# Which engine turns the attention outputs of four units: TensorE or the transposing DMA

## The chip, the cores and the metric

The kernel runs on one core of a Trainium2 chip. The metric is device time in microseconds (us). The core has five engines with queues of their own: TensorE (PE; its weight loads are shown apart as PEld), VectorE (DVE), ScalarE (ACT), GpSimd (POOL) and SyncE (SP), which here only issues DMAs. Sixteen DMA engines move the data.

## The reference

The inputs are q, k and v with 8 batches, 8 heads, 576 positions and 64 features per head, and two weight matrices, 512 x 2048 and 2048 x 512. Attention is computed twice: on averages of four neighbouring positions, and locally with a band of three positions to each side. Both results are added, and a dense part follows.

```python
def sm_attn(qq, kk, vv):
    s = scale * np.matmul(qq, kk.transpose(0, 1, 3, 2))
    s = s - np.max(s, axis=-1, keepdims=True)
    a = np.exp(s)
    a = a / (np.sum(a, axis=-1, keepdims=True) + 1e-09)
    return np.matmul(a, vv)
...
out_up = np.repeat(out_d, factor, axis=2)          # out_d = sm_attn of the averages, factor 4
...
scores = np.where(mask, scores, -1000000000.0)     # mask: |i - j| < 4
...
return (out_up + out_local).astype(np.float32)
...
h = x @ w_in                                       # x: 4608 tokens x 512
g = h - np.tanh(h)
return (g @ w_out).astype(np.float32)
```

## The kernel before

The work is cut into 32 *units*, each one batch and two heads: units 4b to 4b+3 are batch b. A unit goes through these steps (`attention`, L490 to L802):

- q and k are loaded by SP (L358, tiles st; some in Tw), cast to bf16 (L516, qr) and turned so that features lie on partitions: in units 0 to 7 by TensorE (L523), from unit 8 on by a transposing DMA (L567, kq; L561 for the remainder rows rr of a batch, which are loaded at L370 into sr and cast at L506).
- the averages' q and k are formed (L604, L609 and others), TensorE forms the scores (L667, L677, L683; these matmuls use 64 rows), ACT the exponentials (L688, L692, L696, tile E), DVE or GpSimd multiplies by the band mask (L723).
- TensorE multiplies by v (L737; v is loaded at L382, cast at L442, and averaged by L473 on TensorE or L454 and L458 elsewhere). DVE takes the reciprocal of the sums (L753) and normalises into `ln`, six blocks of 128 x 128 with tokens on partitions (L755).
- ln has to be turned so that features lie on partitions, and the local result and the average's result are added into `xT`, in two instructions (`join`, L773).

The last step has two forms, chosen per unit by the table `BACK`. With 1, TensorE turns the six blocks into PSUM (L780), ACT or DVE copies the averages' part to SBUF (`od`, L784 or L786), and DVE joins from PSUM. With 0, SP issues one transposing DMA from ln to `lT` (L792), and DVE or GpSimd joins from SBUF:

```python
lambda: nc.sync.dma_start_transpose(
    out=lT[s].rearrange("p (n c) -> p n c", c=128),
    in_=ln[s].rearrange("p n c -> p (n c)"))
```

The tiles ln, lT, od and E have two buffers each, used by even and odd units.

The dense part of batch b (`mm1`, L814) multiplies the 512 main tokens of the batch, from xT, by w_in in 16 groups of four matmuls with 512 columns; ACT takes tanh (L826), DVE subtracts (L829, tile gT). It needs xT of all four units of its batch. The remaining 64 tokens of two batches go together (L841, L852, L854). The second product runs for the batch before in the meantime: plain (L895) for batch 0, from batch 1 on with seven products of half size (L1035; the sums of quarters that it needs are made by L944 and L970, the results put together by L1056, L1059 and L1106); L867 is that of the remaining tokens. Stores are issued at L925 and L883.

No loop sets the order. Every step is recorded as an operation with what it reads and writes, and four tables of text then say everything else: `TURNS` is the order in which all 2,199 operations are emitted, for all engines and SP's queue; `ENGINES` picks an engine for each operation that has a choice; `BANKS` picks the PSUM bank; `FILL` places idle matmuls (L1244, on a tile of zeros), and `BEHIND` adds waits between certain operations. Each engine works its own instructions in this order, and SP issues its DMAs in it, so that an instruction that waits holds what stands behind it on the same engine.

Of the kernel before, what the change touches and what calls it, by code (L numbers as in the profile page):

```python
# [101 lines left out]
def kernel(  # L102
# [44 lines left out]
    REL = [  # L147
# [4 lines left out]
    ]  # L152

    TURNS = (
        "0003070G0H0I0J060E0F0K0L04050Q0R0O0P0W0X010e0f0C0M0N0S0T100Y0Z110g0h020a0b1215130D0A160U"
        "0V171H1P18141I0B1J190m0n1L1Q1A1K1R221M1N0i0j1O242R231T1j1k1B251S1C1f1g1u1U0c0d1W1v1w2S1y"
        "0k0l1x2Z091V2I2J0y2T082G2H1z1D2V291E2W0o0p261F1d1e2U1X1l1m212X27201n1o2z1Y2b1Z0z391p1q2a"
        "0q0r2d282c2n2o1r1G2e311h1i1s2f2p2q2g2A2K2L322Y1t3A3B2B2O2y5H2C3C3D302D2P3G5I332E1a353E0s"
        "0t2M2N5J34362v2h2F373N3O5K5L5P2i1b5e5f380u0v3F5M5S2w5N2r2s2j5O5Q3H5U5R3I3J5v662Q2k683K5B"
        "5T1c635E5V3L3d2l5C5x2m643j3k5y3M3l3e5D5F3f3g5X3p3q5W0w0x3m3h3v3r3n3w3i3P3Q5w3s5Y3t2t2u3o"  # L160
        "413x615k5l3y3u5z3z4243604744404D4E4548623T3U495Z654A464F4G4B4J6b5a4K4H4L4M3V3W674N4C6e4P"
        "6c6B4Q5g5h4I4R4S2x694V3R3S4O4W6g4b5b6T4X4c5c6A4T4Y5d4h5s4Z4U6V4i6U4j5t5m5n4k4a4d4e4l4n6W"
        "3X3Y4o4f4p4q4m6C6d4r6X6D4t6Z4u6E6Y4v7A4w4z6a505G4g51526F7B536f6G554s4x3Z3a56576Q6j6H3b3c"
        "587f7C6h7g6R54597D7E4y887F6i8d7G895A7I7H8e6k5u966l976m6y9C736z6n717J7475728E7K7l7L7m7677"
# [12 lines left out]
        "9R9SDPDVErEsDQDLJxDWDpDRDXJRDbG7G8FuEGDcDYG5G6DkDdDqFXFYDlGJIQDeDmGOIiIjJSEZGTDnDrDsGUFd"
        "GHMvMwFLGZFvGIINGcIOGhGiGaHhFmHmGbGuFMEtGnFNF6GzGsH0FwFOFPGAFxH5IuIqHrHAIRFyFzIvHCJ1ITHD"
        "ISJ2HIGBGCGtHNIxIyIVHwHSJ3IUHUJkJlJ4FQHVIkIlHaJ5JGJHG0IWJ7JEJFJ6HfIIJTJUGDIXIrGEHgHBGKGF"
        "IYJoJpGLIzJ8IoIpGMJXGGGPKLKMJ0GQGNK0K1GVJyJ9GWJAGRGdJYIsItGeGXGSHTJZGfGYGjJbGkJaGgJMGoHx"  # L180
        "JzGvJVGpGlK6K2K3GwGqI0K7I5JdGmMYIZIaIAGxGrMZIBJWH1MWGyJqJrH2ICH6JOJPH3JNH7JBJCJsK8H8JcHE"
        "KAHFImInJtK9K4HJJuJvH4NAHKKCJmJnJeH9IbMaMbHGHOJfHPHLHHMeHWK5KJKKHMHXHbJKJLJgMfHcHQHiHYKB"
        "HRJhJiHjMgHdHZHnHkMrMsHeHsMhMzN0HtHlHoMtMuHuKuKDHpI1I2HvKRM4I3NBM5HqMcMAJDNCNDMiI6KEI7I4"
        "KZNGKTKUI8KaKFJIJJJQKbKcDgDhNHMdI9KwKGKHKxKSL2KvMkL3IDIEMXKhMjKiKjL9KkMlLAKpLPMmJwNhKsKt"
        "LQMnKqKrLVNgLWNZNaJjNILbMBN5NiNjNEN6LdNKKILeNJLjNbNTNULkNMNLN7N8KVMxMyLpKWNmNNKPKQL8QmLr"
        "N1N2KXNnLsOCNdNeNFLBNOQnMoMpNPLCLqLHNkLIKYNlOFOGLxOLNoLNKdLOKNKONsLyRDREKlNqM3KmOMNQNRNp"
        "KeMGODKyKnONOEKfKoMJLcOHOIOPKzKgOOL4MKNrNVNWL0L5N3N4OQLDL6MPO1O2L1N9NcLENzO0MqMQL7LFRLRM"
        "NtORLGLJO7LKNuNvLRO8LLLSNSOJLXLMNwNxLTLYMROSOKQwLULfLlOTLZLgOUV1LtQxLhLuLaOVOWLmRTLiQyLv"
# [12 lines left out]
        "WfWiWWWsWxWoWlWOWpWyWqWPWjWrWtWgX4WhXAXqWbX5WwX6XFX1X3X7X8WzXNWuX0XSX9WvXEXXXJXOXBXKXLXC"
        "XMXPXGXfXQXTXDXgXkXhXRXUXWXYXVXbXrXHXlXcXsXIXvX2XiY0XZXdXmXaXeY5XtXjXuXwY1XnYAY6XxYFYbXy"
        "YGXzY9YEY2YHXoY3YIYBYJYCYOY4YPYcYdYDYKYQYLYRYSXpYMYNYTYUYVYeYWYfYgYXYYZ2YZYaYjYkY7Y8Z3Yi"
        "YlYwYxYyYhYzYmZ0Z4Z5YnZ7YoYpZ1YqZ6YrZAZ8Z9YsYvZBYtYuZCZDZJZEZKZHZFZGZOZIZPZQZRZSZLZMZN"
    )
    ENGINES = (
        "APADDADAADPPDDPPDDADDDDAPPDADDAADDDPDDDDDAADDAPAADDDAAADDDPPAPPPAADAPPPDDDAAPADADPPPPDAA"
        "PADAAAPPPDDAPDPDAAPPDPDAAAADPPAADDAADDDDDPDPDDPPDAAAPPAAPPDDAAPPPAAPPDDPPADDDDDPPPAPPAAP"
        "PDPPPAPPAAPDDPDDAPDAADPDDPDAPDPAADPDDDPDDDDDPPPAPPAAPPDPPPADDAADDDPPPAPPAAPPDDDDAPPPDADD"
        "PDPPADDDDDDDPAPPAAPPDPDDAPPAAPPDPDPAPPAADDDDPPPDPPAADPDPPPDDDDDDPPAPPAAPPDPPPAPPAAPPDPPP"  # L210
        "APPAAPPDDPDADPDAAPPDDDPADDDDDPPPADPAAPPDPDDAPPAADPDPPPDPAADDDPPPPPDDDDPPPAPPDDD"
    )
    BANKS = (
        "0123453012067016731120212706021330112130022310312010301210031220313200320131002302101322"
        "1203320110023110230110023110012310201302020100121030123101321321310021010113021310213211"
        "0301213001210301230110210123110321132010310213021031032011003210310121021010120031010210"
        "1010300123001230012301230123746524173025604276540257613"
    )
    FILL = (
        "15717 2b71 2A71 3B41 2D11 5S31 3H31 6671"  # L220
    )
    BEHIND = (
        "0211 1H12 1D1V 0z20 1t2f 5I30 5Q5N 635B 5w5W 6562 7H6i 7271 9UCH ABAA AmAF DtAL BiCJ F7C"
        "Z FgEm IHFJ IPG9 JxFt EtGb IrJ6 MYK7 NAK4 KRKu NhLA QnOC OMLO NcOQ OXNy V2Oo RYR1 RZP7 O"
        "BP8 SVSU SdSW V6V5 R8TR RkVZ VmVz VlWE"
    )

    const = ctx.enter_context(tc.tile_pool(name="const", bufs=1))
# [257 lines left out]
    def attention(p):  # L486
# [276 lines left out]
        def join(eng, loc, pool):  # L763

            for t0, step, nt, n, o in ((1, 28, 3, 28, 144), (0, 114, 2, 30, 512)):
# [7 lines left out]
                eng.tensor_tensor(out=dst, in0=src, in1=add, op=ALU.add)  # L773
        if BACK[p]:
            bname = ("bk", p)
# [500 lines left out]
```

## Time and profile before

| what | value |
|---|---|
| median of 3 runs | 311.13 us (311.07 to 311.53) |
| the profiled execution | 311.1 us, its span 309.4 us |
| granted TensorE clock | 1.0 |
| busy PE, DVE, ACT, POOL | 299.1, 248.2, 213.5, 165.0 us |
| transposes L780 on TensorE | 72 matmuls, 219 ns each (units 0 to 11) |
| transposing DMAs lT<-ln, L792 | 20 (units 12 to 31) |
| first L814 starts, last TensorE instruction starts | 30.16 us, 305.44 us |

The table's busy times come from the profile page, the clock from the list of cores, and the starts from the timeline. A matmul's time counts until its result is out, while the next one starts earlier: matmuls with 512 columns are shown with 379 ns each, and follow each other at a distance of 216 ns. A step's share of TensorE's time is therefore read from the distance of starts.

### The profile page before, as it was taken

The page shows a single profiled execution, that of the slowest core. Times are in us where ns is not written, and L with a number is a line of the kernel's source. Part 1 is how long each engine was busy: PE and PEld are TensorE (multiplying, and loading weights), DVE is VectorE, ACT ScalarE, POOL GpSimd, SP SyncE. Part 2 cuts the span into 40 slices and gives each one's busy share as a digit, 9 for nine tenths or more (in the row PEclk, how much of TensorE's full clock was granted, in tenths as well). Part 3 has the DMA queues.
Part 4 walks back from the last instruction along what each step waited for, and adds up shares of the span by engine and source line. Part 5 has one row for each costly group of instructions (what it writes and reads, how often), then busy time and mean ns, then how long its engine had stood idle before and what let it go on. Part 6 is the DMA issues. An engine that isn't in the chain of part 4 may idle for free.

```text
span 309.4 us, 7786 instructions
## 1 busy us (share of the span) xinstructions
PE 299.1 (97%) x2969; PEld 198.6 (64%) x2980; DVE 248.2 (80%) x450; ACT 213.5 (69%) x380; POOL 165.0 (53%) x213
## 2 busy tenths in 40 slices
PE   8878999999999999999999999999999999999995
PEld 3656555455677666875587665657868655567784
DVE  2687887689998889999897888989897987745644
ACT  2778776288888777988966977887768875445210
POOL 5437795026764476338761477485553580517900
PEclk9999999999999999999999999999999999999999
DMA  7999999999999999999999989999998733000134
GB/s 223 249 246 237 242 243 166 206 219 258 253 244 286 228 216 301 219 230 221 201 219 277 224 192 207 261 270 270 173 251 152 174 95 95 0 0 3 51 122 136
DMA packets 120870, 60.81 MB, mean 197 GB/s; under 512 B 88832, under 2 KB 118528, under 8 KB 120832
## 3 DMA queue, kind: packets, MB, share of 16 engines
q1 hardware_dynamic: 115968, 55.53, 78.3%
q0 software_dynamic: 4224, 4.19, 8.5%
q10 hardware_dynamic: 640, 0.59, 0.6%
q8 instruction: 23, 0.38, 0.5%
q14 instruction: 15, 0.12, 0.1%
HBM read 44.04 MB, written 9.44 MB: 173 GB/s over the span
## 4 chain that ended last, share of the span: by engine, by line
PE 90%; DMA 3%; SPq 3%; DVE 1%; issue 1%; ACT 0%; DVEq 0%; ACTq 0%
PE ps L814 36%; PE ps L1035 28%; PE ps L737 5%; PE ps L841 5%; PE ps L867 4%; PE ps L895 4%; PE ps L667 3%; SPq L382 2%; DMA st<-in_k_dram 2%; DMA sr<-in_k_dram 1%; PE ps L780 1%; PE ps L683 1%; SPq L358 1%; PE ps L473 1%; PE ps L677 1%
## 5 line engine op out<-in xcount | busy, mean ns | idle before, releaser
L814 PE MATMUL ps<-xT,w_in_sb 128*128 128x512 bf16 x512 | 122.4, 379 | 0.0
L829 DVE TENSOR_TENSOR gT<-ps,u 128x512 bf16<-128x512 f32 x128 | 84.6, 685 | 19.0 <-ACT u L826 18.3
L826 ACT ACTIVATE u<-ps 128x512 f32<-128x512 f32 x128 | 74.5, 601 | 33.4 <-PE ps L814 29.7
L814 PEld LDWEIGHTS <-w_in_sb 128*128 128x128 bf16 x512 | 47.9, 98 | 46.9
L1035 PEld LDWEIGHTS <-gT 128*128 128x128 bf16 x672 | 64.4, 98 | 15.8
L1035 PE MATMUL ps<-w_out_sb,gT 128*128 128x256 bf16 x336 | 43.4, 273 | 0.0
L1035 PE MATMUL ps<-Tw,gT 128*128 128x256 bf16 x336 | 42.8, 273 | 0.0
L516 POOL CAST qr<-st 128x512 bf16<-128x512 f32 x40 | 24.1, 615 | 20.6 <-DVE gT L970 6.2
L688 ACT ACTIVATE E<-ps 128x912 bf16<-128x912 f32 x32 | 29.7, 930 | 3.0 <-PE ps L677 2.2
L755 DVE TENSOR_TENSOR ln<-ps,r 128x768 bf16<-128x768 f32 x32 | 30.6, 956 | 1.0 <-DVE r L753 0.2
L594 ACT COPY kt<-kq 128x576 bf16<-128x576 bf16 x23 | 27.2, 1188 | 0.7 <-DMA kq<-qr 0.5
L737 PEld LDWEIGHTS <-E 128*128 128x128 bf16 x576 | 21.4, 97 | 5.3 <-DVE E L723 0.8
L723 DVE TENSOR_TENSOR E<-E,mask 128x1152 bf16<-128x1152 bf16 x29 | 23.5, 813 | 1.4 <-ACT E L688 0.7
L773 POOL TENSOR_TENSOR xT<-lT 128x336 bf16<-128x336 bf16 (+1 forms) x24 | 15.9, 684 | 14.8 <-DMA st<-in_k_dram 4.7
L604 POOL TENSOR_TENSOR half<-kq 128x576 f32<-128x576 bf16 x15 | 19.2, 1281 | 5.9 <-DVE v L454 1.8
L696 ACT ACTIVATE E<-ps 128x576 bf16<-128x576 f32 x32 | 20.8, 651 | 0.3 <-PE ps L683 0.3
L609 POOL TENSOR_TENSOR qkd<-half 128x288 bf16<-128x288 f32 x21 | 16.8, 799 | 6.9 <-DVE gT L970 4.2
L1106 POOL TENSOR_TENSOR y<-y,keep 128x512 f32<-128x512 f32 x12 | 15.3, 1273 | 9.5 <-ACT y L1056 9.5
L737 PE MATMUL ps<-vw,E 128*128 128x65 bf16 x320 | 18.9, 193 | 1.2 <-DVE E L723 0.8
L1056 ACT COPY y<-ps 128x512 f32<-128x512 f32 x19 | 11.1, 585 | 11.0 <-PE ps L1035 10.7
L854 DVE TENSOR_TENSOR gL<-ps,u 128x512 bf16<-128x512 f32 x16 | 15.8, 1013 | 2.3 <-ACT u L852 2.3
L737 PE MATMUL ps<-vpr,E 128*128 128x65 bf16 x128 | 16.3, 194 | 0.0
(127 smaller groups left out, 469.6 us busy)
## 6 DMA issues: line engine op xcount, KB each, us to landing
vst<-in_v_dram SPq DMA_DIRECT2D x56, 160.0 KB, 4.1
st<-in_q_dram SPq DMA_DIRECT2D x28, 256.0 KB, 4.4
st<-in_k_dram SPq DMA_DIRECT2D x28, 256.0 KB, 5.0
out_dram<-y SPq DMA_DIRECT2D x14, 512.0 KB, 3.6
v<-in_v_dram SPq DMA_DIRECT2D x20, 256.0 KB, 4.0
w_in_sb<-in_moe_w_in_dram POOLq DMA_DIRECT2D x4, 512.0 KB, 9.4
w_out_sb<-in_moe_w_out_dram POOLq DMA_DIRECT2D x4, 512.0 KB, 8.0
vr<-in_v_dram SPq DMA_DIRECT2D x8, 128.0 KB
```

The costliest lines, as they stand in the source:

```text
L516: (eng, ns, lambda dst=dst, src=src, fn=fn: fn(out=dst, in_=src), port)
L594: ("ACT", 1180, lambda: A.copy(out=ktv, in_=src), False),
L604: eng.tensor_tensor(out=half, in0=flat[:, 0:576], in1=flat[:, 576:1152], op=ALU.add)
L688: A.activation(out=E[s][:, :, E0:E0 + 456], in_=at(s1)[:, :, PS0:512], func=AF.Exp, scale=SCALE)
L696: A.activation(out=E[s][:, :, EP:EW].rearrange("p h (i c) -> p h i c", i=2)[:, :, :, 0:G], in_=at(s2)[:, :, 120:408].rearrange("p h (i c) ...
L723: eng.tensor_tensor(out=el, in0=el, in1=mask.unsqueeze(1).to_broadcast([128, 2, S]), op=ALU.mult)
L737: T.matmul(po[:, hh, 65 * n:65 * n + 65], E[s][:, hh, e:e + 128], vv, start=start, stop=stop)
L755: op("DVE", 960, lambda: V.tensor_tensor(out=ln[s].rearrange("p n (h d) -> p h n d", d=D), in0=blocks()[:, :, :, 0:64], in1=r[s].unsqueeze ...
L814: T.matmul(at(name)[:, 0, :], w_in_sb[:, dc, fc * 128:(fc + 1) * 128], xT[dc][:, c0:c0 + S].rearrange("p (c g) -> p c g", c=4)[:, :, 0:128 ...
L826: op("ACT", 600, lambda: A.activation(out=u[us], in_=at(name)[:, 0, :], func=AF.Tanh), reads=[("hd", kb, fc)], writes=[("u", us)], uses=[n ...
L829: op("DVE", 690, lambda: V.tensor_tensor(out=gT[g][:, fc, :], in0=at(name)[:, 0, :], in1=u[us], op=ALU.subtract), reads=[("hd", kb, fc), ( ...
L1035: T.matmul(dst, left[:, f, 128 * j:128 * j + 128], right[:, f, :], start=(first and e == 0 and f == 0 and (j == 0 or apart)), stop=(e == 1 ...
```

## The change

The entries of `BACK` for units 8 to 11 (batch 2) become 0: their six transposes each on TensorE, the copies od and the joins from PSUM are left out, and four transposing DMAs L792 with joins from SBUF take their place.

```diff
-    BACK = [c == "1" for c in "11111111111100000000000000000000"]
+    BACK = [c == "1" for c in "11111111000000000000000000000000"]
...
     TURNS = (
-        "0003070G0H0I0J060E0F0K0L04050Q0R0O0P0W0X010e0f0C0M0N0S0T100Y0Z110g0h020a0b1215130D0A160U"
...
+        "00040O0P0B0I0J0Q0R0K0L0G0H010E0F0g0h030W0X0C0e0f050M0N02100Y0Z1H151I0m0n1J1L0c0d1K221M0o"
...
     FILL = (
-        "15717 2b71 2A71 3B41 2D11 5S31 3H31 6671"
+        "15714 1351 1771 2T41 1E71 1X51 2b71 2h71 5S41"
```

The other tables are new as a whole: TURNS, ENGINES, BANKS and BEHIND differ from the first entry on, so every engine's order differs, in the opening as well as in the units that the change of BACK doesn't touch. The number of operations is the same in kind apart from the step described; TensorE has 2,954 matmuls in place of 2,980 (24 transposes and 2 fillers fewer), SP issues 250 DMAs in place of 246. Line numbers of the changed kernel are one lower behind the tables.

What stands differently around the places of the change: of the four new joins two are on DVE and two on GpSimd; L784 (od on ACT) occurs 5 times in place of 1, and L786 (od on DVE) 3 times in place of 11; masks on DVE 30 in place of 29. SP's first loads are those of unit 1 and then unit 0, in place of 0 and then 1, and GpSimd issues three of the four loads of w_in one after the other, where casts stood between them.

More of the change, by code (lines that the diff above doesn't have):

```diff
@@ L160 @@
[L160 to L164, printed above, removed]
@@ new lines @@
+        "0p1116231O13121N1714240k0l181P19091A0A0U0V2S1R1Q250S0T1T2R0D0a0b082T1u262V2U1S1j1k1W071f"
+        "1g06391B1C2W1U2G2H1v1w270i0j1D1y1x2Z1l1m1z1d1e0y2X201V2I2J1E291n1o1F282z1X1h1i2a211p1q3A"
+        "2Y2b0z3P3Q2c1Y2d1Z0q0r1r2n2o315e5f2e0s0t1s2g1G2A3N3O0u0v2f3B2y2p2q3C303D332t2u5H2B3E2O2C"
+        "341a3G322D2M2N351t2P3F2h1b372v365P5J1c2w382i5I5S5Q2j3H2E2Q5K2F2k5U5R5E3I3J5L5B2l5T5N5C5F"
+        "3K2K2L5X5D2m3d3e3L5V3f3M3j0w0x3p5M3k3q5W3r5O3g3l3m3h5v5Y3n3i643v3w3x3o3y633s413z5Z42655a"
@@ new lines @@
+        "433t445x47485y406T495b456U3u662r2s4A614D5c6b4J4B5d4K4E46684F4G4L5w5g5h4C674H4M3V3W5k5l4P"
+        "4V4N4W3T3U3X3Y4Q6B4R4O3R3S4S6V4T6X4I5m5n4X4Y694b5i5j4U2x4h6W4i5z6Y4j4Z4c604k4n6A624d4e4l"
+        "6e6Z4o4a5G6g4p5s4m4t6c4u6a4v4f5t4q6d4z504r4g6C7B6f6D4w7A6E51554x523Z3a566j574y6F3b3c5853"
+        "4s6Q7f6h7C7g596G6i886H6R7D547E897F5A8d8e5u72967I6k737G8E716l76776y7l6z7m7H7475976m8j9T7J"
+        "9U9V6K6L9C7K9D7L5q5r8k6I6J6n6s6t7M6o8p5o5p7N6p7r7O6O6P8q787s6M6N9f798F8K9g6u6v8vCB8w9a6q"
@@ new lines @@
+        "6r8L8xCC9h9v9w9i7X9jCF6w6x7YCG9t9u7x9k7Z8Q9Z8R6S7a9b9c9I8S9l7y9W9mCE7b7R7S9X7hCD7V7W7z9n"
+        "7P7Q70AB7c9o7i9x9y9pAA7d9JBD7jACAD7n7e7o9YCH9O9d9P9q9rCI7p7t7kA7AG9eAdA3A4A87u9QB4B5807v"
+        "AH817qB0B1Ae84829zA0Ah85AgA1A2AI83868A7T7U9s7wAJ8BAiAj878GAK8HAEAL8MAVAW8I8NAFATAUAM8V8J"
+        "B2B3AoAm8CANBGBHAq8D8ZAn8WAO8OAP8aBFAp8X8f8PDtAQAR8b8gBE8YAk8l8h8mBM8cBIBJ8rAr8i8s8n8yAs"
+        "8T8UAt8zAbAc8t928oDxBcBdAu908uDyEHEI93AlBN919899AvDuAw9E94AS9F9A9K95AxAyBKBOEb9GBP9L9BEa"
@@ new lines @@
+        "A9DzE0BqE3Br9M9HBsBQB8B9BtE49NCLBaBbBRBAAXAYBTByBSBzELEMBLCJC0A5A6C1EPEQCMBBCKC6E5E6CRE7"
+        "C9CACSC7C8CYE1BUEcEdCZE2CoBVCpAzBWCuE8CvEABXBYE9D0EiDvAfD2EJEKD3BiEkD8BeBfBjEgD9AZAaEBEh"
+        "DEBkBlEVEjENEODGIFElF7EuEvDHCXEmDMB6B7EnDNF8EeCaBZF9FAEfCbECCgFDEDBmEwExBCBuDSG3G4BvEWBn"
+        "IgIhFEBwC2FeBoC3IGFhFiBxFfFFC4FGChBpF2FICNERESFHC5FgCTCnCUFjFkFKCOCmCcFJCdFTFUCVEoF3EXEY"
+        "CPCWCiD19R9SCeCjCQIcIdCqCrDFCfF4F5CkCwBgBhCsEpCxClIeIfD4IHFBCtCyD5EEEFDAEqFnD6DBDTDCCzDU"
@@ new lines @@
+        "IJFlDZD7IKFCDaDDDIFoDODfDwFpIwFqDVFrFZILIMDJIPDPFsFaDKDiETEUFtDjFuEyEzDWMUDQDLDoIQF0F1Dp"
+        "DXDRFXFYG9DbFRFSDqDcEGDkG5G6DdDYDlErEsFLDeDmJSGJFMF6JxGODnFbFcGTEZG1G2GHGUG7G8FvGZIiIjGI"
+        "HhINDrDsGcIOGhGaGiGnGbGuGsFNIvGzFmH0EtFwH5FOFPFxHmHAHrGtFdIRFyFzHwITHCJ1IVFVFWHDISGAHIIx"
+        "IyJ2HNJRJ3IqHSIUJTJUJ5HUJ7FQHVJ4HaJkJlG0HfIkIlIWIuJ6IsItGDIIHgGKKLKMIrGLJyIzJGJHIXIYGEGM"
+        "HTGBGCGPGFJEJFGQGNJ8IZIaJXGRGGGVJ0GWJ9JAGdJYGeGXGSMVJZGfJzGYGjJaMWK2K3GkGgGoGlHxHBGpK0K1"
@@ new lines @@
+        "JVGvGmGqI0JMGwJWMzN0JNI5K6IADgDhJbIBIoIpGrK7GxH1H2JdMYGyH6H3JsICH7K8MZH8HEJcMaMbK9HJK4HF"
+        "H4MeKCJeJoJpH9HGHKJOJPHOMfJfHLImInHHHPKAHWJmJnIbHMHQHXJKJLHbK5HRJBJCHiKBJgHjHYHcIDIEHnHZ"
+        "HdJuJvHoHkHeMgMtMuNAHsHpHlKJKKJtHtMkMrMsKuI1MiI6JIJJHuI2HqNBJQKDJDNCNDI7McHvM4I3M5I8KRI4"
+        "KNKOMAMdKZJhJiKSKaI9NGKbMhKcKTKUKEKFKhNHJwKiKjMjKGKHKkKvKwKpKxKPKQNEL2KqKrL9NFL3JqJrMlLA"
+        "MxMyLPMmNgLQKsKtMnLVNhNTNULWJjMBLbNIN5LdN6NiNjNJKILeLjNKOCLkNMMvMwNLKVNZNaLpKWNmNNRDREL8"
@@ new lines @@
+        "OELrN7N8KXNOLsNPMoMpNnMXLxLyLqNkKYLBN3N4M3NoNbLCMGNqLHNsNcNdNeLIOLNlOFOGKdKlOMKeLOLNNVNW"
+        "KmNpKyNQNRODKzKnNrMJONO1O2L0KoLcMKOHOIOOL1MPMQKfO7NtN1N2MRN9QmL4OcOdKgO8L5ORNzO0QnLDNuMq"
+        "L6NvO9OALJLKOPLEL7LLNwNxLROQLFLXLSLGNSRHRILYLTOSLMOJLfOTOKQwLgLULlOULmLZQxLtLhLaOVOWLuRT"
+        "QyLnLiOgLzLvLoM0QrOiOjR0M6LwM1HyHzQqM7MCM2NyQsQtM8MDMLM9MEMMRSR2OqMFOhRURVOvMNOXP0QzP1MO"
+        "RFRGOkP6OoOlRBRCOrNfOaObOwOpOmOsNXNYOxOYOZOtP9OnRlRmQoQuPEOySHSIPFOuPKQvRNR9RAOzP2O5O6RO"
@@ new lines @@
+        "PAPPP7PBRnRoPGRPRQPCR1P3MSMTPHPDRYP4O3O4PLPIR3P5RWPSRZR4RXPMR5S4PYPTPJR6R7PNPZS5RaPUPOPd"
+        "PaRyPVPeRcRzPlPbPfPqOBS0S1RbPmPgPvP8PwPnMHMIQ3RdReRpRqQ4PxPoPrOeOfRtS6SqSrPsPySUPRQ5PtPW"
+        "RuSXSYS7Q8PQPXPcQpSJSKQFV6SNSOPhRfSVS2Q9SdS3PjPkQ6SeQGQAPpV1SARgV2PuRhSWQKS8PzR8QLSZSaQB"
+        "SfQ1SgV5SLSMQ2S9Q7RJRKSjQCSPSsStQHQEQ0QDSwSxQJQMQORvRwSbQNQTV3V7V8SBQUQPPiQQSuSvSCQIQYRi"
+        "RjQRQZVUSDQXQaVBQcQSSESFRRQhQiShVTQbQdScRLRMQeVCT6SRSSQjSQT7QfSyQkQlTTQgVDRrRsSzTUT0T1VE"
@@ L226 @@
+        "3 IQMU IvGb IrJ6 NBKu NgLA OENm LcNr NSOQ QoOp RYR1 RtRd Q0SP RkVG VOVa VmVz VlWE"
     )
```

75 lines of the change are left out of this document (19 added, 56 removed).

## The prediction

> **What bounds the kernel now.** I read the busy table and the slices first, then the chain that ended last, then the waits of TensorE, and last the timelines around the places that the change touches.
>
> ```profile
> PE 299.1 (97%) x2969; PEld 198.6 (64%) x2980; DVE 248.2 (80%) x450; ACT 213.5 (69%) x380; POOL 165.0 (53%) x213
> PE   8878999999999999999999999999999999999995
> DMA  7999999999999999999999989999998733000134
> PE 90%; DMA 3%; SPq 3%; DVE 1%; issue 1%; ACT 0%; DVEq 0%; ACTq 0%
> ```
>
> TensorE carries 90% of the chain. Busy time alone would not say so (a busy row counts a matmul until its result is out), so I looked at the stretches: from 30 us to 305.7 us TensorE is busy practically without a hole, and the longest of its waits are these.
>
> ```profile
> 0.00:30.00 30.00, 23.86 (x323) 16.09 (x326) 19.05 (x62) 19.21 (x41) 15.41 (x34) 1.00 0.99 240
> 60.00:100.00 40.00, 39.84 (x410) 24.99 (x411) 37.16 (x67) 34.02 (x61) 21.45 (x29) 1.00 1.10 250
> 100.00:260.00 160.00, 159.90 (x1604) 107.61 (x1606) 141.37 (x232) 125.36 (x214) 90.41 (x122) 1.00 0.98 218
> ...
> PE ps L1244 <- DVE lT L1166: 1.3, 1, 1.3
> PE ps L737 <- DVE E L723: 0.8, 1, 0.8
> PE ps L546 <- ACT E L688: 0.8, 1, 0.8
> ```
>
> The columns of the stretches are length, then busy time of PE, PEld, DVE, ACT and POOL, the granted clock (1.00), the DMA share and GB/s. All ten waits of PE lie in the first 30 us (the opening), which hangs on loads, ACT and DVE. The first matmul of the dense part, L814, starts at 30.16, the last PE instruction at 305.44: these 275.3 us are pure TensorE work, and 3.9 us of last stores follow. So there are two terms: when L814 can begin, and how much TensorE work stands behind it, plus whatever stalls come in anew.
>
> **Parts of the change.** *Removed from TensorE:* four groups of six transposes (L780), those of units 8 to 11.
>
> ```profile
> 96.24 0.50 PE L780 MATMUL ps<-ident,ln 128*128 128x128 bf16 x6
> 96.67 0.39 PE L667 MATMUL ps<-kq,kt 64*128 64x112 bf16 x8
> 96.99 0.51 PE L780 MATMUL ps<-ident,ln 128*128 128x128 bf16 x6
> 97.33 1.91 PE L1035 MATMUL ps<-Tw,gT 128*128 128x256 bf16 x16
> ```
>
> The price of a group is not 0.50 us but the distance to the next start: 97.33 - 96.99 = 0.34 us (six starts 56 ns apart); the 0.43 us before L667 holds some 0.1 us that L667 takes at any place, since its 64-row operands follow a 128-row matmul. Four groups: 4 x 0.34 = -1.36 us, all of it on the path.
>
> *Moved in TensorE's order.* The order of all engines is new. I counted TensorE's instructions up to the first L814 in both orders, at their start distances in the trace (512 columns 216 ns, 256 columns 109, 128 columns 56, L737 30, the paired score matmuls 28). Without fillers, 12.73 us stand ahead of it before and 12.50 us after, so 0.23 us slip behind it. Of the 38 places where TensorE goes over to the scores and back, two more now lie behind the first L814; such a place costs 96 + 124 ns of extra start distance in the trace: +0.4 us. Work behind the first L814: -1.36 + 0.23 + 0.43 = -0.70 us. The two fillers that are gone and the 17 that are now 14 at the start lie in the opening, where TensorE waits anyway.
>
> *The opening.* What holds it is the end of the chain before 30 us:
>
> ```profile
> 17.36 4.54 DMA sr<-in_k_dram
> 22.02 0.48 issue
> 22.50 0.94 ACT E L688
> ...
> 27.11 0.69 DVE ln L755
> 28.12 0.97 DVE ln L755
> 29.14 0.51 PE ps L780 x6
> 30.76 2.82 PE ps L814 x13
> ```
>
> ACT casts batch 1's remainder rows (sr) ahead of unit 3's exponentials, so these wait for that load until 22.50. In the changed order ACT does the same thing in the same place, and on SP's queue the bytes up to that load are the same 4.7 MB (it stands 21st, not 22nd): 22.5 again. From there I added up DVE's new list by its rows: mask of unit 2, two casts that wait for a load at some 21.5, unit 1's normalisation, then mask, three joins and two normalisations until unit 3's is done. It ends at about 28.8 us (29.08 before). Between that and L814 the old order put the scores' tail and L473 (30.16 - 29.08 = 1.1 us); the new one goes from unit 3's transposes straight to L814 (0.45 us). That makes 29.25, or -0.9 us. Against it, GpSimd now issues three of the four w_in loads in a row, where the first stood at 19.12 and the second at 23.83; if that takes from SP's loads, unit 3's exponentials come later, by up to the 2.8 us that ACT once waits for such a load. Bounds -1.3 to +1.9 us; I take -0.5, nearer the DVE sum, since only the start of w_in moves and not what shares the engines.
>
> *Moved on DVE, ACT and GpSimd.* Four copies od (224 ns, L786) go, and four joins read SBUF in place of PSUM. Joins on DVE cost the same either way, on GpSimd more:
>
> ```profile
> L773 POOL TENSOR_TENSOR xT<-lT x24: 601/686/771, 120.7 to 254.8; 128x336 bf16<-128x336 bf16 x12, 128x240 bf16<-128x240 bf16 x12
> L773 DVE TENSOR_TENSOR xT<-lT x16: 274/302/336, 133.8 to 259.3; 128x336 bf16<-128x336 bf16 x8, 128x240 bf16<-128x240 bf16 x8
> DMA to landing us min/median/max: 2.8/4.4/5.3
> ```
>
> Of the four new ones two are on DVE and two on GpSimd (2 x 0.69 us each), whose share is 53%. The new tables flip other choices too (one more mask and one more small token sum on DVE, four more od on ACT), and DVE's total by rows comes out within 2 us of the old one. None of it is on the path while TensorE has work: 0.
>
> *Added on SP's queue:* four transposing DMAs, some 1.24 us of SP each, 5 us of SP's 306. Each waits for ln, and the loads behind it on SP wait with it.
>
> ```profile
> SPq L792 <- DVE ln L755: 10.4, 6, 3.2
> ```
>
> Six of the twenty in the old kernel waited, 1.7 us each on average; four more would hold the queue up to 4 x 1.7 = 7 us. Cover: before any load is needed there are several others in flight, TensorE never waited for one after 30 us, and SP's loads end at 250 us. On the engines a lone transpose shows as a share of 0.80 for 1.4 us (from 256.5 us), 1.1 us of all sixteen, so four take 4.5 us of a stretch (60 to 100 us) that is full (1.10). Gone, the cover would cost up to these 4.5 us; I take 0 to 0.1 as in the twenty units that already go this way without a stall.
>
> [...]
>
> *Sum:* -0.70 - 0.5 + 0 = -1.2 us against the profiled execution's 311.1 us (span 309.4, 1.7 us around it; the median of the runs is 311.13): **309.9 us**.
>
> **Rivals.** *First, slower: the dense part of batch 2 waits for unit 11.* With TensorE turning, its last join ended 0.8 us ahead of L814 (98.32 against 99.08). Now ln must go through SP, DMA and the join. In the new order unit 11's values stand 8.4 us ahead of batch 2's first L814 (5.6 before). Reciprocal 0.23, ln 0.96, then eleven DVE instructions that sum to about 5.3 us by their rows, then the join 0.55; with the values' own 0.55 us some 0.4 us is left. The DMA has those 5.3 us; unit 15, the nearest row, took 130.27 to 134.24 (4.0 us) from ln's end to the join. The point from which it decides: landing later than 5.7 us after ln's end. If the SP queue first has to issue unit 14's transpose, which stands shortly ahead (1.24 us of issue, and a wait for its casts, of which SP's longest for GpSimd's qr was 1.2), and landing takes the longest 5.3 us, that is 1.24 + 1.2 + 5.3 = 7.7, a stall of 2.0 us, and the same at one other batch would double it: 309.9 + 2.0 to + 4.0, **311.9 to 313.9 us**. For it: DVE is 93% busy between 60 and 100 us. Against it: batches 5 and 6 ran with joins that ended 0.57 and 0.30 us ahead, without a wait.
>
> *Second, no change: the opening comes later.* w_in in front of the opening's loads, +0.9 in place of -0.5: 311.1 - 0.7 + 0.9 = **311.3 us**. For it: 3% each of the chain are DMA and SP, all there. Against it: the DVE list above.
>
> *Third, slower: DMA becomes the bound.* 4.5 us more of engine time arrive in the full stretch and are not won back; every later unit is late by part of it, and TensorE waits ahead of the dense parts: 309.9 + 2 to 4.5, **312 to 314.4 us**. Against it: from 200 us on the DMA share falls, and the last load ends 50 us ahead of the end.
>
> *Fourth, more than forecast:* the opening gives its full -1.3: **309.1 us**.
>
> **How the numbers follow.** Forecast 0.47 and fourth rival 0.15, first 0.12, second 0.17, third 0.09. The forecast's own range is 309.1 to 310.4 (opening -1.3 to 0). Reaching into the second rival and the near end of the first, the range is **308.9 to 311.9 us**; 2 in 10 is left out, nearly all above. A measurement of this kernel can tell 0.2%, 0.6 us, from no change: faster (below 310.5) 0.62, same 0.17, slower (above 311.7) 0.21.
>
> **What would show it.** L780 x48 and not x72; 24 transposes L792 on SP. The first L814 at 29 to 30 us: later than 31 is the second rival. From there to the last PE start 274.6 us (275.3 before): more by x us means x us of stalls, and the waits of PE then name them. A wait of L814 on xT near 101 us is the first rival; waits of PE or ACT on st or kq after 100 us the third. SP's waits for ln should grow from 10.4 us by 3 to 7. The forecast is wrong if TensorE's waits after 30 us exceed 0.5 us in total.

## The result, and the profile after

The changed kernel takes 315.31 us (median of 4 runs, 313.89 to 317.57) against 311.10 (310.35 to 311.53): a ratio of 1.0138, 95% interval 1.0104 to 1.0172. It is slower by 4.2 us in the medians where 1.2 us less were forecast. The profiled execution took 315.4 us, its span is 313.6.

First the page of the changed kernel, in the lines that answer to those of before: busy times, two rows of slices, and the shares of the chain that ended last.

```profile
PE 300.8 (96%) x2954; PEld 198.3 (63%) x2954; DVE 251.2 (80%) x446; ACT 213.6 (68%) x381; POOL 164.4 (52%) x212
...
PEclk9998999999999999999999999999999999999998
DMA  7999999999999999999899999999895343000054
...
PE 76%; DMA 7%; SPq 6%; DVE 4%; POOL 2%; issue 2%; ACT 2%; ACTq 0%; POOLq 0%; DVEq 0%
```

TensorE is busy for 1.7 us more although it has 15 matmul records fewer, and its share of the chain has fallen from 90% to 76%: DMA and SP's queue now hold 13% of it, not 6%. Apart from the last slice, with the last stores, one slice of the granted clock is no longer full, the fourth. The stretches show where (columns as before):

```profile
0.00:30.00 30.00, 23.33 (x311) 15.71 (x311) 18.48 (x61) 19.79 (x43) 14.15 (x32) 0.98 1.03 241
60.00:100.00 40.00, 38.53 (x382) 22.86 (x380) 37.40 (x56) 32.53 (x57) 20.24 (x27) 1.00 1.08 230
100.00:260.00 160.00, 158.97 (x1605) 107.91 (x1603) 142.45 (x238) 125.33 (x212) 89.02 (x119) 1.00 0.99 219
```

Between 60 and 100 us TensorE is without work for 1.5 us (0.2 before), between 100 and 260 for 1.0 (0.1 before). The first product of the dense part (L814 of before, L813 here) starts at 30.72 us (30.16 before), the last TensorE instruction at 309.65 (305.44): from the one to the other 278.9 us, where 275.3 stood before and 274.6 were forecast.

*The opening.* TensorE's instructions there, with the wait ahead of each in brackets, and then the same time in windows of 3.41 us:

```profile
26.67 0.51 PE L779 MATMUL ps<-ident,ln 128*128 128x128 bf16 x6 [0.16 <-DVE ln L754]
28.62 0.68 PE L472 MATMUL ps<-vw,pick 128*128 128x128 bf16 x5 [1.44 <-POOL vw L441]
...
30.11 0.82 PE L779 MATMUL ps<-ident,ln 128*128 128x128 bf16 x6
30.72 0.63 PE L813 MATMUL ps<-xT,w_in_sb 128*128 128x512 bf16 x1
```

```profile
21.85:25.26 3.41, 2.76 (x51) 2.38 (x49) 3.38 (x9) 2.86 (x8) 0.39 (x1) 1.00 1.14 194
25.26:28.67 3.41, 1.80 (x36) 1.26 (x34) 2.84 (x8) 2.77 (x8) 1.86 (x4) 1.00 1.19 241
28.67:32.09 3.42, 3.42 (x25) 2.17 (x25) 1.81 (x8) 1.10 (x3) 3.19 (x5) 0.50 1.18 246
```

DVE did finish unit 3's ln early, at 28.17 us. But the new order puts L472 of unit 4 (the pooling of its v) ahead of unit 3's transposes; that v was issued at 19.48 us, landed 8.21 us later, and TensorE stood 1.44 us for it. Behind it the clock is granted at 0.50 for 3.41 us: L472 takes 0.68 us (0.45 at full clock), and the first dense products start 427 ns apart, not 216.

*The full stretch.* All waits of ACT, DVE, GpSimd and TensorE on a DMA between 75 and 112 us, first in the kernel before, then (the longest, and the longest of TensorE) in the changed one; the columns are total, times, longest:

```profile
POOL qr L516 <- DMA kq<-qr: 0.3, 1, 0.3
...
POOL qr L516 <- DMA st<-in_k_dram: 0.2, 1, 0.2
```

```profile
POOL qr L515 <- DMA st<-in_k_dram: 2.2, 3, 1.2
ACT vw L441 <- DMA vst<-in_v_dram: 2.2, 1, 2.2
POOL xT L772 <- DMA lT<-ln: 1.8, 2, 1.0
POOL half L603 <- DMA kq<-qr: 1.6, 1, 1.6
DVE xT L772 <- DMA lT<-ln: 1.5, 1, 1.5
ACT vw L441 <- DMA st<-in_q_dram: 1.3, 1, 1.3
...
PE ps L1034 <- DVE gT L969: 0.7, 1, 0.7
...
PE ps L666 <- ACT u L825: 0.4, 1, 0.4
```

Before, the engines waited 0.5 us for DMAs there; now 11.4 us, 3.3 us of it for lT itself and the rest for what stands behind it in the queue. TensorE waits for no DMA: it waits for ACT and DVE, which stand in order behind instructions that wait for one.

### The profile page after: what moved, and what is told of

Same layout as the page of the kernel before. It is cut to its first block, busy times and chain, and to the rows that moved or that the text cites. A ratio compares the mean times of both kernels' runs of the same rounds, so it can differ in the third digit from the quotient of the medians.

```text
span 313.6 us, 7725 instructions
## 1 busy us (share of the span) xinstructions
PE 300.8 (96%) x2954; PEld 198.3 (63%) x2954; DVE 251.2 (80%) x446; ACT 213.6 (68%) x381; POOL 164.4 (52%) x212
## 4 chain that ended last, share of the span: by engine, by line
PE 76%; DMA 7%; SPq 6%; DVE 4%; POOL 2%; issue 2%; ACT 2%; ACTq 0%; POOLq 0%; DVEq 0%
PE ps L813 33%; PE ps L1034 25%; PE ps L894 4%; PE ps L736 4%; DMA vst<-in_v_dram 3%; SPq L381 3%; PE ps L840 2%; PE ps L866 2%; SPq L357 2%; PE ps L666 2%; DMA sr<-in_q_dram 2%; DMA rT<-rr 1%; DMA st<-in_q_dram 1%; DVE gL L853 1%; PE ps L682 1%
## 5 line engine op out<-in xcount | busy, mean ns | idle before, releaser
L813 PE MATMUL ps<-xT,w_in_sb 128*128 128x512 bf16 x512 | 121.3, 381 | 0.3 <-DVE y L1058 0.3
L828 DVE TENSOR_TENSOR gT<-ps,u 128x512 bf16<-128x512 f32 x128 | 83.6, 683 | 18.1 <-ACT u L825 17.4
L813 PEld LDWEIGHTS <-w_in_sb 128*128 128x128 bf16 x512 | 48.0, 98 | 49.9 <-issue 1.4
L1034 PE MATMUL ps<-Tw,gT 128*128 128x256 bf16 x336 | 41.6, 273 | 1.6 <-DVE gT L969 0.9
L1034 PE MATMUL ps<-w_out_sb,gT 128*128 128x256 bf16 x336 | 42.6, 273 | 0.0
L772 POOL TENSOR_TENSOR xT<-lT 128x336 bf16<-128x336 bf16 (+1 forms) x28 | 19.0, 700 | 14.8 <-DVE E L722 8.5
L722 DVE TENSOR_TENSOR E<-E,mask 128x1152 bf16<-128x1152 bf16 x30 | 25.0, 834 | 1.5 <-ACT E L687 0.8
L603 POOL TENSOR_TENSOR half<-kq 128x576 f32<-128x576 bf16 x14 | 17.9, 1277 | 14.5 <-DVE r L752 7.7
L441 ACT CAST vw<-vst 128x640 bf16<-128x640 f32 x22 | 15.9, 732 | 6.4 <-DMA vst<-in_v_dram 5.1
L853 DVE TENSOR_TENSOR gL<-ps,u 128x512 bf16<-128x512 f32 x16 | 15.7, 1024 | 3.2 <-ACT u L851 3.1
```

The costliest lines, as they stand in the source:

```text
L722: eng.tensor_tensor(out=el, in0=el, in1=mask.unsqueeze(1).to_broadcast([128, 2, S]), op=ALU.mult)
L813: T.matmul(at(name)[:, 0, :], w_in_sb[:, dc, fc * 128:(fc + 1) * 128], xT[dc][:, c0:c0 + S].rearrange("p (c g) -> p c g", c=4)[:, :, 0:128 ...
L828: op("DVE", 690, lambda: V.tensor_tensor(out=gT[g][:, fc, :], in0=at(name)[:, 0, :], in1=u[us], op=ALU.subtract), reads=[("hd", kb, fc), ( ...
L1034: T.matmul(dst, left[:, f, 128 * j:128 * j + 128], right[:, f, :], start=(first and e == 0 and f == 0 and (j == 0 or apart)), stop=(e == 1 ...
```

## The experiments

For the runs that are compared by their dense part, three numbers beside the ratio: the start of the first dense product, the time from there to the last TensorE start, and the waits of the four engines on DMAs between 75 and 112 us (all their waits together). The clock column says from when it was granted at half, and for how long, before the last stores. The three numbers and the clock come from one execution each, and executions of one kernel differ (those of e_pv4 took 312.5 to 316.1 us), so that some tenths of a microsecond in them prove nothing by themselves.

```
run            ratio (95%)            first   to last  DMA waits  half clock
before         1                      30.16   275.28    0.5       -
after          1.0138 (1.0104-1.0172) 30.72   278.93   11.4       28.67, 3.41
e_load_again   1.0119 (1.0074-1.0165) 29.46   277.92    7.6       -
e_free         1.0061 (1.0038-1.0084) 30.48   277.24    6.6       -
e_tiny         1.0076 (1.0042-1.0111) 30.02   276.78    4.9       -
e_tiny_late2   1.0066 (1.0039-1.0093) 29.69   278.14   (later)    -
e_alone        1.0201 (1.0161-1.0240) 30.15   281.40    6.5       105.50, 3.41
e_undo         1.0166 (1.0118-1.0214) 32.94   279.03    0.0       30.23, 6.83
e_pv4          1.0088 (1.0054-1.0123) 30.56   277.20    7.6       17.89, 3.41
e_pv4_undo     1.0106 (1.0068-1.0143) 30.78   277.73    3.0       19.68, 3.41
e_fill         1.0098 (1.0078-1.0117) 30.94   276.58    7.8       19.48, 3.41
e_pv4_less     1.0038 (1.0022-1.0054) 29.81   275.82    0.8       -
e_pv4_soft     1.0160 (1.0119-1.0200) 29.09   277.42    5.7       -
```

**The opening: e_pv4 and e_fill.** e_pv4 is the changed kernel with three entries of its order moved: POOL's cast of unit 4's v (2Q) behind qkd of unit 4, the product L472 of unit 4 and its copy (5E, 5F) behind the fourth dense product.

```diff
 TURNS
-2E2Q5K2F2k5U5R5E3I3J5L5B2l5T5N5C5F3K2K2L5X5D2m3d3e3L5V3f3M3j0w
+2E5K2F2k5U5R2Q3I3J5L5B2l5T5N5C3K2K2L5X5D2m3d3e3L5V3f3M3j5E5F0w
```

> The changed kernel with the pooling product of unit 4's v (L472) and its copy moved behind the fourth product of the first chunk of batch 0's dense layer, and POOL's cast of that v behind qkd of unit 4: no TensorE instruction before the dense layer needs the late vst load. Opening theory: the 1.4 us wait goes, the first L814 starts near 29.3 us instead of 30.7, and the clock is granted in full there: 315.3 - 1.8 to - 2.5 = 312.8 to 313.5 us. Load theory: the stalls after 75 us stay as they are, 3 us and more. If the opening doesn't matter (what is gained there is waited for later): 315.3 us, within 0.5.

e_fill leaves that order and fills the wait:

```diff
 FILL
-"15714 1351 1771 2T41 1E71 1X51 2b71 2h71 5S41"
+"15714 1351 1771 2T41 1E71 1X51 2b71 2h71 5S41 5E16"
```

> The changed kernel with six filler products (6 x 0.216 = 1.3 us, their result is read by nothing) right ahead of L472 of unit 4, where TensorE waited 1.44 us for the late v: the wait is filled with work, nothing else moves. Clock theory (the idle time there is what lets the clock be halved from 28.7 to 32.1 us, and the half clock costs more than the wait): the profile shows the clock at 1.0 there and the time falls by 1.0 to 1.7 us, 313.6 to 314.3. Wait theory (the wait itself is the loss, the clock's dip comes or not as it will): 315.3 us, within 0.5, and the dip stays.

Both come out faster than the changed kernel, with ratios to before of 1.0088 and 1.0098 in place of 1.0138, some 1.6 and 1.2 us; the intervals overlap, so that the gain is likely and not clear of noise. In both the clock is full from 22.9 us on. The window of e_fill that answers to 25.26:28.67 above:

```profile
26.30:29.72 3.42, 3.30 (x49) 2.11 (x47) 3.20 (x9) 2.90 (x8) 3.27 (x5) 1.00 1.18 243
```

TensorE is busy for 3.30 us of it, not 1.80, and no half clock follows. The first product comes no earlier (30.94), and still the dense part is 2.3 us shorter: 0.7 of it is the half clock itself, the rest are fewer waits of TensorE in the full stretch (0.5 us after 31 us, 2.1 in the changed kernel). That is what the clock theory had in time and for the clock; the fewer waits it did not have, and one execution does not show that they hang on the clock. e_pv4 gained less at the first product than expected (30.56, not 29.3): in its execution, as in that of e_fill, the clock was halved earlier, behind another hole (14.48 to 17.89 in e_pv4, TensorE busy 1.48 us of 3.41). How the loads land in the opening differs from execution to execution: e_undo, whose opening is the changed kernel's to the letter, waited 2.8 us at L472 there, stood at the half clock for 6.83 us and began at 32.94.

**Four transposes more, and nothing else: e_load, e_load_again, e_free, e_tiny.** The kernel before, with DMAs added on SP behind ln of units 8 to 11; nothing reads what they write (lT is free for these units).

```diff
+        if 8 <= p < 12:
+            op("SP", 1230, lambda: nc.sync.dma_start_transpose(
+                out=lT[s].rearrange("p (n c) -> p n c", c=128),
+                in_=ln[s].rearrange("p n c -> p (n c)")),     # e_load
+                in_=w_in_sb[:, 0, 0:768]),                    # e_free
+            for i in range(2):                                # e_tiny
+                op("SP", 600, lambda i=i: nc.sync.dma_start(
+                    out=lT[s][:, 64 * i:64 * i + 4], in_=w_in_sb[:, 0, 0:4]),
```

> The kernel before, units 8 to 11 still turned by TensorE, with four transposing DMAs of ln(8) to ln(11) added on SP's queue, as far behind each ln as the changed kernel has them; nothing reads what they write. Load theory (SP's queue and the DMA engines are full from 60 to 103 us, and four more transposes of 1.2 us of issue each push the loads behind them back): the stalls of the changed kernel appear, +2.5 to +3.5 us, 313.6 to 314.6 us, with PE waits between 75 and 105 us. Order theory (the new tables themselves bring the stalls, whatever turns the outputs): 311.1 us, within 0.3. Opening theory (the changed kernel loses its time at L472 of unit 4 before 31 us and to the half clock behind it): 311.1 us, within 0.3.

> The kernel before with the four added transposing DMAs that nothing reads, once more, for a trace of an ordinary execution: 312.9 us (2.05 over before, as measured). Wait theory (what costs is SP standing at a transposing DMA until its ln is written, with the loads behind it): SP's waits for ln grow by 5 us or more. Issue theory (the 1.2 us that each keeps SP issuing): SP's waits for ln stay under 2 us. Engine theory (the 16 DMA engines are full): as the issue theory, and the median time from issue to landing of the loads between 75 and 105 us grows by 0.5 us or more.

> As the kernel with the four added transposing DMAs of ln, at the same places of SP's queue, but each turns 128x768 of w_in_sb, which has long been loaded, so that SP has nothing to wait for at them. Wait theory: 311.0 to 311.3 us. Issue theory and engine theory: 312.5 to 313 us, as with the wait.

> The kernel before with eight small copies of 128x4 values of w_in_sb into lT on SP's queue (two at each place where the transposing DMA stood, some 0.55 us of issue each), with nothing to wait for: SP's issue time without the packets. Issue theory: 312.5 to 313 us. Engine theory and wait theory: 310.8 to 311.2 us.

e_load took 1.0066 (1.0039 to 1.0094) times the kernel before, some 2 us more, a little under the 2.5 to 3.5 of the load theory; its repetition 1.0119. That fells the theory that only the order is to blame. SP's waits for ln did not grow (7.9 us in e_load_again, 10.4 before), and e_free, which has nothing to wait for, costs the same 1.9 us: no wait theory either. And e_tiny costs as much. In the trace its 1,024 packets of 8 bytes take 9 ns each, 0.6 us of all sixteen engines together, against 3.5 us for the transposes' 3,072, most of 18 ns; what it shares with them is SP's issue, 1.1 to 2.0 us at each of four places. The sign that the engine theory named, loads landing 0.5 us later between 75 and 105 us, does not show either: for the six to eight of SP's loads there whose landing is recorded, the median is 4.5 us before, 4.8 in e_load_again, 4.6 in e_free and 4.1 in e_tiny, and the mean DMA share is 1.12, 1.09, 1.10 and 0.98. Counted from the first dense product, next to nothing differs up to 82 us, then 1.5 to 2.6 us are lost by 141, and from there on every dense product stands at a constant distance. Counted so, SP's own DMAs come 2.7 to 4.1 us later at 102 us, in all three. The waits of e_free between 75 and 112 us show the way from there to TensorE:

```profile
ACT kt L595 <- DMA kq<-qr: 2.9, 1, 2.9
...
DVE half L605 <- DMA kq<-qr: 2.0, 1, 2.0
...
PE ps L1042 <- ACT y L1063: 1.6, 1, 1.6
...
DVE vrs L405 <- DMA vr<-in_v_dram: 1.0, 1, 1.0
```

SP hands over kq later, ACT stands at kt, and the copy y behind it, for which TensorE needs the bank, comes late. In e_tiny it is DVE that stands 1.8 us for a late load of v (vr), and gT behind it.

**The change alone, and the change undone: e_alone, e_undo, e_pv4_undo.** e_alone keeps the order of before; e_undo and e_pv4_undo keep the new one (without and with e_pv4's opening).

```diff
-    BACK = [c == "1" for c in "11111111111100000000000000000000"]   # e_alone
+    BACK = [c == "1" for c in "11111111000000000000000000000000"]
-    BACK = [c == "1" for c in "11111111000000000000000000000000"]   # e_undo, e_pv4_undo
+    BACK = [c == "1" for c in "11111111111100000000000000000000"]
```

> The order of before with units 8 to 11 alone turned by DMA: back and od are taken out, the joins of units 8 to 10 stand on POOL some 50 places behind their ln, that of unit 11 on DVE right before batch 2's first dense product. Load theory: -1.4 us of transposes and +2.5 to +3.5 of stalls, 312.2 to 313.2 us. Order theory: 309.7 us, and up to 312 if batch 2's first product has to wait for unit 11's join (5 us from its ln, of which about 3 are covered). Opening theory: as the order theory.

> The order of the changed kernel with units 8 to 11 back on TensorE: four groups of six L780 transposes, od and DVE joins from PSUM, no DMA transpose for these units. Load theory: the stalls between 75 and 105 us go and 1.4 us of transposes come back, 315.3 - 3.0 + 1.4 = 313.7 us. Order theory: the stalls stay, 315.3 + 1.4 = 316.7 us. Opening theory: the opening is untouched, so 1.5 to 2.5 us over the kernel before remain in it in either case.

> The changed order with the opening mended (L472 of unit 4 behind the first dense products) and units 8 to 11 turned by TensorE again. Load theory, by the +2.05 us that the added transposes cost in the order of before: 313.5 - 2.05 + 1.36 = 312.8 us. Order theory: 313.5 + 1.36 = 314.9 us. By either, what is over the 310.9 us of before is the order's own.

e_alone, at 1.0201 some 317 us, is the slowest of the three, beyond both theories, since it pays the load and the first rival's wait:

```profile
PE ps L814 <- DVE xT L773: 2.9, 1, 2.9
PE ps L683 <- POOL qkd L609: 1.6, 2, 1.1
```

Batch 2's first product waits 2.9 us for unit 11's join, and a half clock of 3.41 us follows. The new order does avoid that wait. By its time e_undo is no faster than the changed kernel (1.0166 against 1.0138), as its opening fell out so badly: of its dense part 4.1 us ran at half clock, which costs 2.1 us, against 0.7 in the changed kernel. Without that the dense part is 277.0 us against 278.2, and in the full stretch its engines wait for no DMA at all. With the opening mended the difference is smaller and has the other sign: e_pv4_undo 1.0106 against e_pv4 1.0088, 277.73 us against 277.20 in the dense part, with intervals that overlap. By this pair the turn by DMA is worth 0.5 us in the new order, not 1.36, and some 0.8 us are given back to the load; by e_undo and the changed kernel the load takes 2.6 us (1.36 and 1.3). The rest belongs to the order: with TensorE turning everything, e_pv4_undo still needs 2.45 us more than the old order behind the first product. Of these, 0.66 are the work that was moved there by the prediction's count, 0.3 is L472 of unit 4, which e_pv4's opening put there, and 0.9 are waits of TensorE of 0.2 to 0.4 us; where the other 0.6 lie, no run shows.

**Less load, or elsewhere.** e_pv4_less leaves eight loads out of SP's queue, e_pv4_soft gives five to POOL's.

```diff
+            left_out = 12 <= p <= 14 or (p, i) in ((11, 0), (15, 0))   # e_pv4_less
-            load(500, issue, [("vst", s, i)], 940, 10 * p - 3000 + 5)
+            load(500, None if left_out else issue, [("vst", s, i)], 940, 10 * p - 3000 + 5)
-    SOFT = [c == "1" for c in "0" * 32]                                # e_pv4_soft
+    SOFT = [c == "1" for c in "00000000000011111000000000000000"]
```

> The changed order with the opening mended, with eight of SP's loads between 62 and 100 us left out (one or both heads' v of units 11 to 15: what the outputs of these units are made of is old data, the work on it stays): 8 x 0.55 = 4.4 us less of issue, about what the four transposes of ln added. Issue theory: the stalls from 75 to 112 us go back from some 3.0 us to the 1.3 of before, 313.5 - 1.7 = 311.8 us. Order theory (the stalls are of the new tables): 313.5 us, within 0.4.

> The changed order with the opening mended and the v4 loads of units 12 to 16 issued from POOL's queue in place of SP's: 5 x 0.5 = 2.5 us of issue leave SP, some 5 x 0.8 us come to POOL, the DMA engines have the same bytes. Issue theory: 0.5 to 1 us faster than with SP, 312.5 to 313 us. Engine theory: 313.5 us. If POOL, which casts q and k for the next units, can't bear it: 314 us or more.

e_pv4_less does what the issue theory says: 1.0038 in place of 1.0088, 1.4 us of the dense part won back, waits on DMAs of 0.8 us in place of 7.6. It takes issue and bytes away together, so it doesn't tell these two apart. e_pv4_soft is a miss: its runs lie between 312.2 and 317.5 us, and the dense part of the profiled one is no shorter than e_pv4's.

**Room on SP's queue: e_pull, e_free_pull, e_pv4_pull, e_tiny_late, e_tiny_late2.** From 41.8 to 54.2 us SP issues nothing, as it stands at unit 8's first transpose. Thirteen loads were moved ahead of it (here by their names, in place of the table's entries):

```diff
 SP's queue
-sr(q, batch 2), vst(7), st(8), rT(batch 2), kq(8), st(9), vst(8), ... st(11)
+sr(q, batch 2), vst(7), st(8), st(9), vst(8), ... st(11), rT(batch 2), kq(8)
```

> The kernel before with thirteen loads (q and k of units 9 to 11, v of units 8 to 11 but one) moved on SP's queue ahead of the first transposing DMAs of unit 8, at which SP stands idle for 12.3 us (41.8 to 54.2): 13 x 0.52 = 6.8 us of issue leave the full stretch behind it. Slack theory: SP gets some 6 us of spare time between 55 and 75 us, the short stalls from 75 to 112 us shrink, 0 to -0.8 us: 310.2 to 311.0 us. Engine theory (the 16 DMA engines, which carry w_out from 40 to 54 us, are the limit, and the loads push w_out back): 311.5 us or more.

> The kernel before with the four added transposing DMAs of w_in_sb, which cost 1.9 us, and with the thirteen loads moved into SP's idle 12.3 us. Slack theory: the added 5 us of issue find room, and the four transposes cost 0 to 0.6 us, 310.9 to 311.5 us. Engine theory: they cost what they did, 312.8 us or more.

> The changed order with the opening mended and the same thirteen loads moved ahead of the first transposing DMA of unit 8 (SP stands 10.7 us there). Slack theory: the stalls from 75 to 112 us go back to those of before as they did with eight loads left out, 313.5 - 1.4 = 312.1 us, down to 311.5. Engine theory or order theory: 313.5 us.

All three are slower (ratios 1.0251, 1.0308, 1.0317). SP's queue in e_pull, start and issue time, and one of SP's waits:

```profile
42.82 1.74 SPq L358 DMA_DIRECT2D st<-in_q_dram  x1
44.62 3.35 SPq L382 DMA_DIRECT2D S<-in_v_dram  x2
48.06 4.53 SPq L382 DMA_DIRECT2D vst<-in_v_dram  x1
52.64 2.09 SPq L358 DMA_DIRECT2D st<-in_k_dram  x1
...
62.19 1.32 SPq L561 DMA_TRANSPOSE rT<-rr  x1
63.62 1.23 SPq L567 DMA_TRANSPOSE kq<-qr  x1
...
SPq L382 <- POOL E L723: 4.0, 1, 4.0
```

The loads took 19 us, not 6.8. The engine theory puts that down to the DMA engines, which carry w_out's loads here, and in time it was right; but no run shows how the 19 us divide, since the profile counts 4.0 us of the longest issue (4.53 us, at 48.06) as a wait for GpSimd's mask. kq of unit 8 came 8 us late and TensorE waited 7.4 us. The room won was no use either: e_free_pull still pays 2.0 us more than e_pull in the dense part, 1.7 of them between 92 and 131 us, because SP next stands at kq of unit 10, and everything behind it is as tight as ever.

e_tiny_late and e_tiny_late2 put e_tiny's copies behind units 13 to 16:

```diff
-        if 8 <= p < 12:
+        if 13 <= p < 17:
-                    out=lT[s][:, 64 * i:64 * i + 4], in_=w_in_sb[:, 0, 0:4]),
+                    out=od[s][:, 64 * i:64 * i + 4], in_=w_in_sb[:, 0, 0:4]),   # e_tiny_late2
```

> The eight small copies on SP's queue once more in the order of before, but two each behind ln of units 13 to 16 (some 115 to 150 us) in place of 8 to 11. Slack theory (SP has no spare time from 60 to 103 us but waits for ln later on, so the price of an issue depends on where it stands): 311.1 to 311.5 us. Flat theory (a DMA more on SP costs the same wherever it stands): 312.6 to 313.4 us, as behind units 8 to 11.

> The eight small copies on SP's queue in the order of before, two each behind ln of units 13 to 16 (115 to 150 us), now into od, which these units don't use, so that they wait for no reader of lT. Slack theory: 311.0 to 311.6 us. Flat theory: 312.6 to 313.4 us, as behind units 8 to 11.

e_tiny_late (1.0154) tells nothing: its copies overwrite eight columns of lT, which these units join from, and SP waits 3.2 us for the transposes into it. e_tiny_late2 costs 1.0066, so the flat theory was right and the slack theory wrong: SP's waits for ln at 115 to 150 us are no spare time. The loss lies at the scores there (L684 waits 1.0 us for qkd, L668 0.9 for kt), for whose kq the copies stood ahead in the queue.

**Another queue: e_free_act, e_pv4_act.** The four transposes from ACT's queue:

```diff
-            op("SP", 1230, lambda: nc.sync.dma_start_transpose(
+            op("ACT", 1230, lambda: nc.scalar.dma_start_transpose(               # e_free_act
+            op("SP", 1230, lambda: (nc.scalar if p < 12 else nc.sync).dma_start_transpose(   # e_pv4_act
```

> The kernel before with the four added transposing DMAs of w_in_sb issued from ACT's queue in place of SP's, at the same turns: the same packets for the DMA engines, no issue on SP, 4 x 1.2 us of issue on ACT. Issue theory (the price is paid on SP's queue, whose kq transposes come later by what is put ahead of them): SP's kq stay where they are in the kernel before, and the time is 311.0 us plus what ACT's 4.9 us cost, 311.0 to 312.0. Engine theory: 312.8 us or more, with SP's loads landing later.

> The changed order with the opening mended and the four lT transposes of units 8 to 11 issued from ACT's queue at the same turns. Issue theory: SP's queue is relieved of 5 us, as with eight loads left out: 313.5 - 1.4 = 312.1 us, if ACT bears 4.9 us more; if ACT (85% busy from 75 to 95 us, and the tanh of the dense layer behind the issue) does not, 313.5 to 315 us. Engine theory: 313.5 us or more.

1.0372 and 1.0617, far outside every expectation. A wait of SP's that appears only with the transposes on ACT's queue, here from e_free_act (in e_pv4_act it is 16.4 us in three, for lT<-ln):

```profile
SPq L568 <- DMA lT<-w_in_sb: 14.0, 3, 5.5
```

Three times SP stands up to 5.5 us at kq until the transpose issued by ACT has landed, although kq does not use lT. Why it waits there no run shows; these two traces show only that the wait comes with the second queue. So this pair could not tell issue from engines.

What stands: 5.6 to 5.9 us more of SP's issue in a stretch where it has none to spare cost 1.5 to 2.6 us in the old order, with next to no bytes as well as with many. That the engines' share in it is small is shown for e_tiny's copies alone; for the transposes, whose packets hold the engines longer (most of them 18 ns, those of e_tiny 9), it stays open how the price is divided. No version tried beats the kernel before.

## Why the prediction was wrong

*Removed, 4 x 0.34 us:* right as a count (L779 has 48 records), but with what the load takes back it comes out as 0.5 us (e_pv4_undo against e_pv4, one execution each) or as a loss (e_undo against the changed kernel).

*Moved in TensorE's order, +0.66 us:* not separated by any run; it was added to an order taken to have no waits of its own. That was the gap: beyond the 0.66 us, some 1.0 us (e_undo, without its half clock) to 1.5 us (e_pv4_undo) come with the new order even when TensorE turns everything, 0.7 and 0.9 of them as short waits.

*The opening, -0.5 us:* the DVE sum was right and even modest (28.17 for 28.8), and the counter-risk looked at the right thing, late loads. It went wrong in asking only which of SP's loads unit 3's exponentials need. The first TensorE instruction in the way was L472 of unit 4, whose load came 8.2 us after its issue. That the three w_in loads in a row made it late is not shown: no run moves them, and in the kernel before a load that SP issued at 19.75 us, behind the first of them alone, took 8.25 us too. The first product came at +0.56, inside the bounds; what no bound held is the clock behind the hole, which cost another 0.7 us of the dense part here and 2.1 in e_undo.

*Added on SP's queue and the engines, 0 to 0.1 us:* the step that failed outright. Its cover, "several others in flight" and "the twenty units that already go this way without a stall", was read from an average. SP issues 34.4 us of the 40 between 60 and 100 us already (the sum of its DMA rows in the kernel before), and those twenty units were ordered with their transposes in it. In place of 0 to 0.1 us the four transposes alone cost some 2 us in the old order (e_load, e_free), and the load took 0.8 to 2.6 us in the new one; e_pv4_less won 1.4 back. The bound of 4.5 us held, though it was worked out from the engines' time: what e_tiny paid was SP's issue, with 0.6 us of the engines' time.

*Rivals:* the first (unit 11's join) did not come in the changed kernel, though e_alone shows that it was real for the old order. The second came in sign, at 30.72 us for 30.16. The third, given 0.09, is the nearest: 312 to 314.4 us was worked out for the same place, with the wait on loads; with the second's loss of 1.1 us on top that is 313.1 to 315.5 us, which holds the 315.3 measured. That is in part luck: the third was worked out from the engines' time, which e_tiny does not bear out, and the order's own share stands in neither.

By single executions the 5.4 us between forecast and time divide so: opening 1.06, half clock behind the first product 0.7, and 3.6 in the rest of the dense part. By e_undo, 2.6 of these are the load and 1.0 the order's own. By the pair with the mended opening they are load 0.8, order 1.5, and 1.3 that the changed kernel loses more than e_pv4 (waits on DMAs 11.4 against 7.6 us). How load and order divide them thus stays open within these bounds; that both have a part is what the pairs agree in.

*The signs named:* the first product later than 30 us, 278.9 us where 274.6 would have stood, and TensorE's waits of 2.1 us after 30 us (0.5 allowed) all told against it; SP's waits for ln did not grow (8.2 us, 10.4 before), though 3 to 7 us more were forecast.

## What to carry to other kernels

A DMA that nobody needs soon is not free if its queue is full where it stands (here 5.6 to 5.9 us more of issue cost 1.5 to 2.6 us): count the queue's issue time in that stretch, and look for the next transfer behind it that an in-order engine will stand at. Price a new order by its first late operand, not by the engine that was late in the old one. And a hole in TensorE's work can cost more than its length, by the clock behind it: here a wait of 1.44 us, and 3.41 us at half clock that cost another 0.7.

## What the runs showed of the hardware

*The clock went by windows.* In every trace in which the clock is recorded, the half clock begins a whole number of times 3.41 us after the clock was first granted (28.67 = 4.78 + 7 x 3.413; 17.89 = 4.24 + 4 x 3.413) and lasts one to three times as long (10.24 us in e_pv4_pull). It went with how busy TensorE was in the window before. Of the windows at full clock, all fourteen with 1.60 us of work or less were followed by the half clock (1.48 in e_pv4, 0.56 in e_alone, 1.60 in e_fill), and none with 1.99 us or more was (2.49 in the kernel before, from 26.51). Three lay between, and no threshold parts them: after 1.80 us (the changed kernel) the clock was halved, after 1.73 (e_pv4_act, from 5.89) and 1.81 (e_free) it was not:

```profile
101.41:104.82 3.41, 1.81 (x30) 1.44 (x28) 2.79 (x5) 3.26 (x6) 0.47 (x1) 1.00 1.19 260
104.82:108.23 3.41, 3.40 (x35) 2.08 (x33) 3.38 (x7) 2.57 (x5) 3.23 (x7) 1.00 1.00 216
```

In the changed kernel a wait of 1.44 us was enough, in a window that other holes had brought to 47% idle, while one of 1.60 us in e_free was not.

*SP's issue time was not a constant.* A load of k took 0.4 to 0.9 us to issue between 75 and 100 us in the kernel before, and 2.09 us at 52.64 us in e_pull, where the profile shows no wait for it. The mean DMA share was 1.1 in the one stretch and 1.2 in the other, so the share alone does not tell when an issue takes longer.
